# Attention feeding a two-layer feed-forward block on one core: left keys' values in one pass of 64x32 tiles, hand-overs of PSUM banks on SyncE, a new order of the work

## The chip, the core and the metric

The kernel runs on one core of a Trainium2 chip. The metric is the device time of one execution in microseconds (us). Inputs and output lie in HBM. "PE" is TensorE, "DVE" VectorE, "ACT" ScalarE, "POOL" GpSimd and "SP" SyncE; a row with a "q" behind the engine's name belongs to that engine's sequencer, which issues DMAs and semaphore work. PSUM has 8 banks of 128 partitions x 512 float32 values; TensorE writes there.

## The reference

```
# q, k, v: 8 x 12 heads x 448 x 64;  cap = 30
scores = cap * tanh((q @ k^T / sqrt(64)) / cap)
attn   = softmax(scores)                     # over the keys
x      = (attn @ v), heads side by side      # 3584 x 768
out    = max(x @ w1, x @ w2) @ w_out         # w1, w2: 768 x 1024, w_out: 1024 x 768
```

## The kernel before

**The algebra.** max(x w1, x w2) is relu(x (w1 - w2)) + x w2, so that out = relu(x wd) w_out + x wm, with wd = w1 - w2 (`subtract`) and wm = w2 w_out (`premultiply`, from transposed blocks of w2 that `turn_w2` makes). Both are made once, in the first third of the run. |cap x tanh| is at most 30, so exp needs no maximum taken off. Everything that TensorE multiplies is bf16.

**Attention.** The 96 heads are worked in 48 pairs and 24 quads of two pairs (four heads, the token's number t). The 448 keys are three chunks of 128 and 64 left over; all scores are turned round: partitions are keys, the 448 columns are queries.
- `scores` (S, L477): for a pair and a chunk two matmuls of 64x128 tiles, one per head, side by side. `left` (L, L484 to L490): the 64 left keys of all four heads of a quad, four matmuls of 64x64 tiles that run side by side.
- `tanh` (T, L482), `tanh_left` (TL, L494), `ex` (E, L498) and `ex_left` (EL) run on ScalarE: tanh from PSUM, then exp in place.
- `add` (A, L510) and `add_left` (B) on VectorE add the exponentials of the chunks for the sums of softmax, from quad 3 on. `total` (Y, L535) sums over the partitions with a matmul of ones, into a bank of the "mm" set; for quads 0 to 2 it takes the chunks themselves.
- `invert` (Y1, Y2, Y3; L537 to L548): the sums stand 32 times over in partitions; a transpose of 32x32 blocks, a reciprocal of 128 partitions x 14, and a transpose back (L546) give the inverse of every sum in all 32 partitions of its head.
- `values` (V, u = 0 and 1; L552 to L564): 32 of the 64 dims of four heads at a time. L560 takes the three full chunks, twelve 128x32 matmuls of 448 columns, four heads side by side. L564 takes the left keys with 128 rows as well: the left keys of two heads share the partitions, `vl` holds v for one half of the rows and zeros for the other (memsets, L286 and L287), so that the other head's exponentials are multiplied by zero. So it has four 128x32 matmuls for u = 0 and four for u = 1.
- `normalize` (N, L573) on VectorE multiplies by the inverse and writes x, transposed, as chunks `2q + u` of 128 rows.

The scores, the left scores and the values share two slots of PSUM, two banks each, handed out in turn by one pool (`s_psum`, name "s", bufs=2, L249). The quad's values hold one of them until both normalises are done.

**The feed-forward block.** It is cut into groups (`Group`): stage 1 makes one 128-wide slice of relu(x wd) for the 448 tokens of a batch (6 chunks of 128), stage 2 a 128 x 384 piece of the output (14 chunks). Each group has one of four banks ("mm0" to "mm3"; token O opens it) and ends with ev: relu on VectorE (L618), or a copy on VectorE (L651) followed by a store (st, L633). A chunk is done as two matmuls of 64x128 tiles, one for the upper and one for the lower 64 rows. `M x y n` puts n such steps of group x on rows 0 to 63 beside n of group y on rows 64 to 127, so that two groups run side by side. Both halves of a group add to the same bank, one after the other; between them stands a **hand-over** (H, L604 to L607): a no-op on an engine's queue that waits for the last matmul of one half and for which the first matmul of the other half waits. In the program of before the no-ops stand on VectorE.

**Loads and crosses.** k, q, v and the weights are loaded and cast by POOL's queue (lk, lq, lv, lw1, lw2, lwo). `load_wo` (L355 to L360) cuts each half of w_out into WOP pieces; WOP is 1. `x_rows` picks which rows of w1 and w2 make a chunk. For pairs 0 to 9 TensorE transposes q and k (X, Xh); from quad 5 on `cross` (cr, L444) does it with a DMA transpose on SyncE's queue, after q and k of that quad have landed and the scores of the quad two before, which hold the same buffer, are done. SyncE also issues the stores.

**The order.** The kernel schedules by hand (`manual_schedule`): the string ORDER (from L9) lists all steps, the STEPS dict at the end maps tokens to the functions, and each engine gets its instructions in the order in which the string names them. Semaphores between engines are added by the framework. D (`keep_warm`, L436) multiplies constants while nothing else is there.

Of the kernel before, what the change touches and what calls it, by code (L numbers as in the profile page):

```python
# [9 lines left out]
dm; ms0; ld0 k; ld0 q; ms; lk 1 0; id; lwo 0 0; lk 2 0; lq 1 0; lw2 0; cd k; lk 3 0; cd q; lw2 2; D 3 28;  # L10
Xh 0 0 0; Xh 0 1; D 3 8; lq 2 0; lq 3 0; XCh 0 0; XCh 0 1; S 0 0; S 0 1; T 0 0; T 0 1; D 3 8; S 0 2; T 0 2;
lw2 1; E 0 0 3; lwo 1 0; lk 4 0; Xh 1 0 1; D 3 22; Xh 1 1; D 3 14; XC 1; lv 0 0; W 0 2; lv 0 1; L 0; WC 0;
S 1 0; TL 0; lv 0 2; OP 0 0 3; P 0 0 1; W 2 0; T 1 0; lv 0 3; EL 0; S 1 1; lw2 3; WC 2; S 1 2; X 2 1; T 1 1;
X 3 2; XC 2; T 1 2; lv 1 0; W 1 0; XC 3; E 1 0 2; S 2 0; WC 1; S 2 1; P 0 0 7; T 2 0; OP 2 0 1; P 2 0 2;
PC 0 0; P 2 0 3; E 1 2 3; P 2 0 1; S 2 2; P 2 0 2; T 2 1; PC 2 0; T 2 2; lv 1 1; OP 0 1 2; P 0 1 5; lv 1 2;
P 0 1 3; OP 2 1 0; P 2 1 1; lv 1 3; P 2 1 1; PC 0 1; P 2 1 3; lw2 5; L 1; Y 0 3; TL 1; lq 4 0; V 0 0; lw2 4;
Y1 0; E 2 0 3; V 0 1; Y2 0; lq 5 0; Y3 0; S 3 0; lk 5 0; N 0 0; W 3 1; P 2 1 1; N 0 1; lv 2 0; P 2 1 1; T 3 0;
P 2 1 1; OP 1 0 2; P 1 0 1; WC 3; P 1 0 1; lv 2 1; S 3 1; EL 1; P 1 0 1; PC 2 1; lv 2 2; S 3 2; P 1 0 1; T 3 1;
P 1 0 2; lv 2 3; P 1 0 2; OP 1 1 3; P 1 1 1; T 3 2; P 1 1 1; PC 1 0; P 1 1 1; lk 6 0; X 4 1; E 3 0 2; P 1 1 1;
XC 4; P 1 1 4; lk 7 0; S 4 0; PC 1 1; S 4 1; T 4 0; W 4 0; lw1 5; W 5 2; WC 4; E 3 2 3; OP 3 0 1; P 3 0 1;  # L20
lq 6 0; S 4 2; WC 5; X 5 3; T 4 1; lq 7 0; P 3 0 1; XC 5; P 3 0 1; lw1 2; P 3 0 1; T 4 2; P 3 0 2; lw1 0; L 2;
Y 1 0; TL 2; lq 8 0; V 1 0; lq 9 0; Y1 1; E 4 0 3; V 1 1; lw1 3; Y2 1; Y3 1; S 5 0; N 1 0; P 3 0 1; lk 8 0;
P 3 0 1; OP 4 1 2; P 4 1 1; N 1 1; P 4 1 2; T 5 0; P 4 1 1; lw1 1; PC 3 0; X 6 3; EL 2; sub 5 0; lk 9 0; S 5 1;
S 5 2; X 7 0; T 5 1; XC 6; P 4 1 2; T 5 2; XC 7; P 4 1 1; lq 10 0; S 6 0; sub 2 0; P 4 1 1; OP 5 0 1; P 5 0 1;
E 5 0 2; P 5 0 1; S 6 1; P 5 0 2; PC 4 1; P 5 0 1; lw1 4; P 5 0 3; T 6 0; sub 0 1; OP 4 0 3; P 4 0 2; PC 5 0;
P 4 0 3; E 5 2 3; P 4 0 1; S 6 2; P 4 0 2; T 6 1; OP 3 1 0; P 3 1 2; PC 4 0; P 3 1 1; lv 3 0; P 3 1 2; T 6 2;
P 3 1 2; sub 3 0; lv 3 1; L 3; Y 2 2; lv 3 2; TL 3; V 2 0; lv 3 3; Y1 2; E 6 0 3; V 2 1; Y2 2; lk 10 0; Y3 2;
S 7 0; N 2 0; sub 1 1; X 8 1; N 2 1; X 9 3; T 7 0; XC 8; P 3 1 1; EL 3; S 7 1; XC 9; S 7 2; OP 5 1 2; P 5 1 1;
lk 10 1; P 5 1 1; PC 3 1; P 5 1 1; T 7 1; P 5 1 1; A 3 0 1; P 5 1 2; lk 11 0; P 5 1 2; T 7 2; sub 4 0; O 0 1;
M 0 -1 1; lk 11 1; S 8 0; M 0 -1 1; E 7 0 2; M 0 -1 1; S 8 1; PC 5 1; lq 11 0; M 0 -1 3; A 3 0 2; O 1 3;  # L30
M 1 -1 3; lv 4 0; H 0; M 1 0 1; T 8 0; M 1 0 1; A 3 1 1; M 1 0 1; lv 4 1; O 2 0; M 2 0 2; H 1; B 3 0; E 7 2 3;
M 2 0 1; lv 4 2; S 8 2; M 2 1 1; B 3 1; M 2 1 1; T 8 1; M 2 1 1; lv 4 3; O 3 2; M 3 1 1; ev 0; M 3 1 2;
lk 12 0; H 2; T 8 2; A 3 1 2; M 3 2 2; cr 5; M 3 2 1; ev 1; lk 12 1; O 4 1; M 4 2 1; L 4; M 4 2 1; lq 12 0;
TL 4; Y 3 3; V 3 0; Y1 3; E 8 0 3; lk 13 0; V 3 1; Y2 3; Y3 3; lk 13 1; S 9 0; M 4 2 1; N 3 0; M 4 3 1; lv 5 0;
M 4 3 1; N 3 1; M 4 3 1; O 5 3; M 5 3 2; lv 5 1; T 9 0; H 4; M 5 3 1; ev 2; S 9 1; M 5 4 1; lv 5 2; ev 3;
M 5 4 1; EL 4; M 5 4 1; S 9 2; A 4 0 1; lv 5 3; O 6 0; M 6 4 3; T 9 1; H 5; A 4 0 2; M 6 5 1; lq 13 0; M 6 5 2;
ev 4; O 7 2; M 7 5 1; T 9 2; M 7 5 1; S 10 0; lk 14 0; H 6; M 7 5 1; M 7 6 1; E 9 0 2; M 7 6 1; ev 5; S 10 1;
lk 14 1; M 7 6 1; O 8 1; M 8 6 2; H 7; lq 14 0; M 8 6 1; M 8 7 2; ev 6; T 10 0; M 8 7 1; O 9 3; M 9 7 1;
A 4 1 1; M 9 7 1; lk 15 0; M 9 7 1; E 9 2 3; H 8; S 10 2; ev 7; M 9 8 1; lk 15 1; M 9 8 2; B 4 0; M 9 8 1;
T 10 1; M 9 8 1; lq 15 0; cr 6; M 9 8 1; B 4 1; M 9 8 2; T 10 2; M 9 8 2; A 4 1 2; M 9 8 1; O 10 0; M 10 8 3;  # L40
L 5; Y 4 2; TL 5; V 4 0; Y1 4; V 4 1; E 10 0 3; Y2 4; Y3 4; S 11 0; M 10 9 1; lv 6 0; N 4 0; M 10 9 2; M 8 9 1;
N 4 1; M 8 9 1; lv 6 1; M 8 9 2; H 10; M 8 9 1; S 11 1; lv 6 2; T 11 0; A 5 0 1; M 8 9 3; lv 6 3; O 11 2;
M 11 9 1; A 5 0 2; EL 5; M 11 9 1; S 11 2; M 11 9 1; lk 16 0; ev 8; M 11 10 2; T 11 1; M 11 10 1; ev 9;
M 11 10 1; cr 7; M 11 10 1; lk 16 1; M 11 10 2; T 11 2; M 11 10 1; S 12 0; lq 16 0; M 11 10 1; st 0 0;
M 11 10 2; E 11 0 2; O 12 1; M 12 10 1; S 12 1; H 11; M 12 10 1; lk 17 0; M 12 10 1; M 12 11 2; H 10 2;
M 12 11 1; lk 17 1; M 10 11 2; H 12; M 10 11 1; T 12 0; A 5 1 1; M 10 11 2; lq 17 0; M 10 11 2; B 5 0;
M 10 11 1; E 11 2 3; O 13 3; M 13 11 1; S 12 2; M 13 11 1; B 5 1; M 13 11 1; M 13 12 1; T 12 1; M 13 12 1;
ev 10; M 13 12 3; lk 18 0; A 5 1 2; T 12 2; M 13 12 3; ev 11; M 13 12 1; lk 18 1; L 6; Y 5 0; TL 6; V 5 0;
lq 18 0; Y1 5; st 0 1; V 5 1; E 12 0 3; Y2 5; lk 19 0; Y3 5; S 13 0; M 13 12 1; lv 7 0; N 5 0; M 13 12 1;
O 14 2; M 14 12 2; H 13; N 5 1; lv 7 1; M 14 12 1; M 14 13 2; H 12 2; S 13 1; lv 7 2; T 13 0; A 6 0 1;  # L50
M 14 13 1; M 12 13 2; lv 7 3; M 12 13 1; H 14; A 6 0 2; EL 6; M 12 13 1; S 13 2; M 12 13 1; lk 19 1; M 12 13 2;
T 13 1; M 12 13 1; O 15 0; M 15 13 1; cr 8; M 15 13 1; lq 19 0; ev 12; M 15 13 1; M 15 14 1; T 13 2; M 15 14 1;
ev 13; S 14 0; M 15 14 1; O 16 1; M 16 14 1; E 13 0 2; M 16 14 1; H 15; S 14 1; M 16 14 1; st 0 2; M 16 15 2;
ev 14; M 16 15 1; O 17 3; M 17 15 2; H 16; T 14 0; M 17 15 1; A 6 1 1; M 17 16 3; ev 15; O 18 2; M 18 16 1;
E 13 2 3; S 14 2; M 18 16 1; H 17; B 6 0; M 18 16 1; M 18 17 1; T 14 1; M 18 17 1; B 6 1; M 18 17 1; O 19 0;
M 19 17 2; ev 16; T 14 2; M 19 17 1; H 18; ev 17; M 19 18 3; lk 20 0; A 6 1 2; O 20 1; M 20 18 3; lk 20 1; L 7;
ev 18; Y 6 3; TL 7; V 6 0; Y1 6; lq 20 0; V 6 1; E 14 0 3; Y2 6; Y3 6; lk 21 0; S 15 0; M 20 19 1; N 6 0;
lv 8 0; M 20 19 2; N 6 1; O 21 2; M 21 19 2; lv 8 1; M 21 19 1; H 20; S 15 1; T 15 0; ev 19; M 21 20 1; lv 8 2;
M 21 20 2; A 7 0 1; O 22 3; M 22 20 1; lv 8 3; EL 7; M 22 20 1; S 15 2; H 21; A 7 0 2; M 22 20 1; lk 21 1;
M 22 21 2; T 15 1; ev 20; M 22 21 1; O 23 0; M 23 21 1; cr 9; lq 21 0; M 23 21 1; H 22; M 23 21 1; T 15 2;  # L60
M 23 22 1; S 16 0; ev 21; M 23 22 3; E 15 0 2; M 23 22 1; S 16 1; M 23 22 6; O 24 1; M 24 22 1; T 16 0;
M 24 22 1; H 23; A 7 1 1; M 24 22 1; M 24 23 3; H 22 2; E 15 2 3; B 7 0; M 22 23 1; S 16 2; M 22 23 1; H 24;
M 22 23 1; B 7 1; M 22 23 1; T 16 1; M 22 23 3; A 7 1 2; M 22 23 1; lk 22 0; O 25 2; M 25 23 1; T 16 2;
M 25 23 1; ev 22; M 25 23 1; L 8; ev 23; lk 22 1; M 25 24 1; TL 8; Y 7 3; V 7 0; lq 22 0; Y1 7; st 1 3;
E 16 0 3; V 7 1; Y2 7; lk 23 0; Y3 7; S 17 0; M 25 24 1; N 7 0; lv 9 0; M 25 24 3; N 7 1; M 25 24 1; lv 9 1;
M 25 24 2; T 17 0; M 25 24 1; A 8 0 1; S 17 1; lv 9 2; M 25 24 2; O 26 0; M 26 24 1; A 8 0 2; EL 8; M 26 24 1;
lv 9 3; S 17 2; M 26 24 1; H 25; M 26 25 1; lk 23 1; M 26 25 1; T 17 1; H 24 2; M 26 25 1; M 24 25 1; cr 10;
M 24 25 1; H 26; M 24 25 1; lq 23 0; M 24 25 1; T 17 2; M 24 25 1; S 18 0; M 24 25 2; E 17 0 2; M 24 25 1;
S 18 1; O 27 3; M 27 25 1; ev 24; M 27 25 2; M 27 26 2; ev 25; M 27 26 3; T 18 0; M 27 26 1; A 8 1 1;
M 27 26 3; st 1 4; M 27 26 1; B 8 0; E 17 2 3; M 27 26 1; S 18 2; O 28 1; M 28 26 1; H 27; B 8 1; M 28 26 2;  # L70
T 18 1; M 28 27 2; H 26 2; A 8 1 2; M 28 27 1; M 26 27 2; T 18 2; M 26 27 2; lk 24 0; L 9; Y 8 2; TL 9; V 8 0;
# [132 lines left out]
def kernel(  # L204
# [11 lines left out]
    nc = tc.nc  # L216
    f32 = mybir.dt.float32
# [14 lines left out]
    NX = 10  # L232
    KB = 2
    VB = 2
    QB = 2
    NS = 3
    W2T = 4
    WOP = 1
    R7 = S // 64
    OB = 4  # L240
    scale = 1.0 / (D ** 0.5)

    ctx.enter_context(tc.manual_schedule())
    const = ctx.enter_context(tc.tile_pool(name="const", bufs=1))
# [490 lines left out]
```

## Time and profile before

| | before |
|---|---|
| median of 3 runs | 339.29 us (338.48 to 340.11) |
| the profiled execution | 338.55 us |
| its span, first to last instruction | 336.7 us |
| mean granted clock of TensorE | 0.999 |
| TensorE busy | 324.5 us, 96%, 4096 matmuls |
| ScalarE busy | 275.0 us, 82% |
| VectorE busy | 228.6 us, 68% |
| GpSimd busy | 173.5 us, 52% |
| chain that ended last | PE 76%, DMA 10%, DVE 5%, ACT 4% |
| DMA | 45.90 MB, mean 136 GB/s |

The span counts from the first instruction to the last; the execution's time has 1.85 us more around it. Busy time of an engine is the union of its instructions; matmuls that run side by side on different tiles count once there, and in the groups by line each with its own length. In a timeline a row has the start (us from the span's start), the length, the engine, the line, the operation, what it writes and reads, and the number of instructions that it stands for; "[1.54 <-PE s L490]" means that the engine had been idle for 1.54 us until that matmul released it. A group by line has min/median/max ns of one, the time of first and last, and what it waited for.

### The profile page before, as it was taken

The numbers are of one execution on the slowest core, as the hardware profiler recorded it, in microseconds if no ns is written. First come the engines' busy times: TensorE is split into PE (matmuls) and PEld (weight loads), VectorE is DVE, ScalarE is ACT, GpSimd is POOL, SyncE is SP. The second block draws the span as 40 slices with busy tenths as digits, with TensorE's granted clock in tenths as the row PEclk, the third lists the DMA queues.
The fourth block names the chain that finished last, engine by engine and source line by source line (L and its number), as shares of the span: only waits on it lengthen the run. The fifth ranks groups of instructions, "written<-read, shape, count | busy, mean of one in ns | idle before, by whom it ended". The sixth has DMA issues, their size and how long they took to land.

```text
span 336.7 us, 9698 instructions
## 1 busy us (share of the span) xinstructions
PE 324.5 (96%) x4096; PEld 198.0 (59%) x4096; DVE 228.6 (68%) x410; ACT 275.0 (82%) x267; POOL 173.5 (52%) x249
## 2 busy tenths in 40 slices
PE   7799999999999999999999999999999999999994
PEld 6545555555766555656665564557675556559662
DVE  2337779786797659758777768767976678675321
ACT  4879999999989998998899998999899989910000
POOL 6547499967774661792855258398438302000000
PEclk9999999999999999999999999999999999999999
DMA  8999999999999999999999999999999983031033
GB/s 148 204 171 156 256 246 72 151 136 169 159 147 132 140 141 140 182 99 180 187 140 65 133 116 224 132 153 177 144 128 138 182 123 47 2 96 47 2 95 93
DMA packets 136077, 45.90 MB, mean 136 GB/s; under 512 B 116321, under 2 KB 131041, under 8 KB 136033
## 3 DMA queue, kind: packets, MB, share of 16 engines
q0 software_dynamic: 96288, 25.08, 77.7%
q1 hardware_dynamic: 39440, 19.86, 31.1%
q8 instruction: 32, 0.52, 0.7%
q10 hardware_dynamic: 304, 0.33, 0.3%
q14 instruction: 13, 0.10, 0.1%
HBM read 47.45 MB, written 11.01 MB: 174 GB/s over the span
## 4 chain that ended last, share of the span: by engine, by line
PE 76%; DMA 10%; DVE 5%; ACT 4%; issue 2%; POOL 0%; SPq 0%; POOLq 0%; DVEq 0%; ACTq 0%
PE mm L597 49%; PE s L477 8%; PE s L560 6%; DMA wo_sb<-in_moe_w_out_dram 5%; PE mm L402 4%; DMA qkT<-kqs 4%; ACT e L498 3%; PE s L490 2%; PE s L564 2%; PE mm L535 1%; PE mm L592 1%; DMA out_dram<-osb 1%; ACT e L482 1%; PE mm L429 1%; DVE osb L651 1%
## 5 line engine op out<-in xcount | busy, mean ns | idle before, releaser
L482 ACT ACTIVATE e<-s 128x896 bf16<-128x896 f32 x144 | 127.5, 930 | 1.9 <-PE s L477 1.9
L498 ACT ACTIVATE e<-e 128x2688 bf16<-128x2688 bf16 (+2 forms) x72 | 122.9, 1708 | 0.0
L597 PE MATMUL mm<-wo_sb,gT 64*128 64x384 bf16 x864 | 116.2, 323 | 0.0
L597 PE MATMUL mm<-wm_sb,xT 64*128 64x384 bf16 x648 | 102.1, 323 | 0.0
L597 PE MATMUL mm<-xT,wd_sb 64*128 64x448 bf16 x768 | 98.9, 349 | 1.0 <-DVE gT L618 0.8
L328 POOL DMA_DIRECT2D kqs<-in_k_dram x76 | 55.8, 737 | 71.3 <-DMA qkT<-kqs 68.7
L597 PEld LDWEIGHTS <-gT 64*128 64x128 bf16 x864 | 60.4, 94 | 24.0 <-issue 0.4
L597 PEld LDWEIGHTS <-wd_sb 64*128 64x128 bf16 x768 | 55.4, 94 | 20.8 <-issue 2.4
L597 PEld LDWEIGHTS <-xT 64*128 64x128 bf16 x648 | 51.0, 94 | 18.4 <-issue 1.0
L477 PE MATMUL s<-qkT 64*128 64x448 bf16 x288 | 55.4, 354 | 2.2 <-ACT e L482 1.8
L618 DVE TENSOR_SCALAR gT<-mm 128x448 bf16<-128x448 f32 x64 | 39.5, 622 | 13.6 <-PE mm L597 13.1
L651 DVE COPY osb<-mm 128x384 f32<-128x384 f32 x54 | 29.7, 555 | 24.3 <-PE mm L597 23.2
L510 DVE TENSOR_TENSOR esum<-e 128x896 bf16<-128x896 bf16 x42 | 26.1, 621 | 23.9 <-ACT e L498 18.3
L346 POOL DMA_DIRECT2D vp<-in_v_dram x48 | 30.4, 638 | 22.0 <-PE s L564 15.9
L328 POOL DMA_DIRECT2D kqs<-in_q_dram x38 | 36.9, 972 | 4.3 <-PE mm L402 3.1
L560 PE MATMUL s<-e,vp 128*32 128x448 bf16 x576 | 35.7, 352 | 0.0
L494 ACT ACTIVATE el<-s 128x896 bf16<-128x896 f32 x24 | 22.0, 917 | 16.4 <-PE s L490 15.9
L477 PEld LDWEIGHTS <-qkT 64*128 64x128 bf16 x288 | 17.2, 94 | 26.7 <-issue 13.8
L661 ACT COPY osb<-mm 128x192 f32<-128x192 f32 x1 | 0.3, 319 | 36.5 <-DMA out_dram<-osb 36.5
L346 POOL DMA_DIRECT2D vl<-in_v_dram x48 | 29.4, 620 | 0.6 <-PE s L477 0.5
L573 DVE TENSOR_TENSOR xT<-s,inv 128x448 bf16<-128x448 f32 x48 | 27.8, 620 | 2.6
L510 DVE TENSOR_TENSOR esum<-esum,e 128x896 bf16<-128x896 bf16 x42 | 26.2, 624 | 1.8
(56 smaller groups left out, 265.8 us busy)
## 6 DMA issues: line engine op xcount, KB each, us to landing
out_dram<-osb SPq DMA_DIRECT2D x54, 192.0 KB, 4.2
vp<-in_v_dram POOLq DMA_DIRECT2D x38, 160.0 KB, 5.3
kqs<-in_q_dram POOLq DMA_DIRECT2D x47, 112.0 KB, 5.7
kqs<-in_k_dram POOLq DMA_DIRECT2D x76, 56.0 KB, 4.0
osb<-in_moe_w_dram POOLq DMA_DIRECT2D x4, 512.0 KB, 9.1
wo_sb<-in_moe_w_out_dram POOLq DMA_DIRECT2D x2, 768.0 KB, 9.2
gT<-in_moe_w_dram POOLq DMA_DIRECT2D x6, 256.0 KB, 7.4
xT<-in_moe_w_dram POOLq DMA_DIRECT2D x2, 512.0 KB, 6.2
```

The source lines that it names most:

```text
L328: nc.gpsimd.dma_start(out=to, in_=x)
L346: nc.gpsimd.dma_start(out=to, in_=x)
L477: nc.tensor.matmul(s[:, h, :S], k_of(t, o, h, j), q_of(t, o, h))
L482: nc.scalar.activation(expo[i][:, 2 * j : 2 * j + 2, :], slots[i, j][:, :, :S], AF.Tanh, scale=scale / cap)
L494: nc.scalar.activation(left_e[t], slots[t][:, :, :S], AF.Tanh, scale=scale / cap)
L498: nc.scalar.activation(e, e, AF.Exp, scale=float(cap))
L510: nc.vector.tensor_add(d, e[:, 0:2, :] if j == 1 else d, e[:, 2 * j : 2 * j + 2, :])
L560: nc.tensor.matmul(ps[r, u, :S], vp[t % VB][:, m, j if turned_by_pe(t) else 2 * j, u::2], expo[2 * t + o][:, 2 * j + h, :], start=(j == 0) ...
L573: nc.vector.tensor_mul(x, vals[t][:, u, :S], sums[t, 3])
L597: ins = nc.tensor.matmul(self.ps, w[r], x[r], start=first, stop=self.at == [self.n, self.n]).ins
L618: nc.vector.tensor_relu(gT[b // 2][:, f, cs], ps)
L651: nc.vector.tensor_copy(o[:, hs], ps)
```

## The change

- **Left values.** `values_left` (VL) does the left keys of a quad for both u in one go: eight matmuls of 64x32 tiles, four heads times two halves of the dims, each with the 64 rows of its own head, into eight different places of 64 rows x 32 columns of the array. It comes ahead of the full chunks and starts the sums (start=True); `values` only adds (start=False) and takes chunks j0 to j1. So `vl` needs no zeros, and its memsets go.
- **Places.** For that to fit, u = 1 has its heads' results in other partitions: `place(m, u)` is R32[m ^ 2u], lower and upper 64 partitions exchanged. Odd chunks of x therefore have their halves exchanged, and so must the rows of w1 and w2: `load_rows` loads the odd chunks in two DMAs of 64 rows. The inverses are needed in both arrangements: Y2b copies the reciprocals with the halves exchanged (two copies of 64 partitions x 14 on VectorE), Y3b is a second transpose of 32x32 blocks.
- **Left scores** are eight 64x32 tiles as well, instead of four 64x64.
- **Slots.** The two PSUM slots of scores and values have names, and which step takes which is written down (TURN), not handed out in turn.
- **Hand-overs** are no-ops on SyncE, not on VectorE.
- **w_out** comes in four DMAs (WOP = 2), not two.
- **keep_warm** keeps a bank that nobody else took (`idle`).
- **ORDER** is new throughout: another front (the first 20 us), other places for the groups' steps, hand-overs and crosses, VL and the split values in the quads, and 134 hand-overs instead of 131. A quad of both orders (quad 6's cross; quad 4's values):

```
before:  M 9 8 1; T 10 1; M 9 8 1; lq 15 0; cr 6; M 9 8 1; B 4 1; M 9 8 2; T 10 2; M 9 8 2; A 4 1 2; M 9 8 1;
         O 10 0; M 10 8 3; L 5; Y 4 2; TL 5; V 4 0; Y1 4; V 4 1; E 10 0 3; Y2 4; Y3 4; S 11 0; M 10 9 1; lv 6 0;
         N 4 0; M 10 9 2; M 8 9 1; N 4 1;
after:   M 8 6 1; H 7; cr 6; lk 15 1; S 10 2; B 4 0; M 8 6 1; M 8 7 1; E 9 2 3; M 8 7 1; B 4 1; lq 15 0; M 8 7 1;
         O 9 1; M 9 7 2; H 8; ev 6; M 9 7 1; T 10 2; M 9 8 2; A 4 1 2; M 9 8 2; L 5; ev 7; VL 4; TL 5; Y 4 3;
         V 4 0 0 2; Y1 4; V 4 1 0 2; E 10 0 3; V 4 0 2 3; Y2 4; V 4 1 2 3; Y3 4; S 11 0; M 9 8 1; lv 6 0; M 9 8 1;
         Y2b 4; M 9 8 1; N 4 0; M 9 8 2; lv 6 1; M 9 8 2; Y3b 4;
```

The diff, without the order's text:

```diff
-    WOP = 1
+    WOP = 2
...
-    s_psum = ctx.enter_context(tc.tile_pool(name="s_psum", bufs=2, space=PSUM))
+    s_psum = ctx.enter_context(tc.tile_pool(name="s_psum", bufs=1, space=PSUM))
...
     def fill_const(eng, i):
-        eng.memset(vl[i][64:, 0::3, :], 0.0)
-        eng.memset(vl[i][:64, 1:3, :], 0.0)
...
+    def load_rows(eng, to, w, c):
+        x = w.rearrange("(q p u) n -> q u p n", p=P, u=2)[c // 2, c % 2]
+        if c % 2 == 0:
+            eng.dma_start(out=to, in_=x)
+            return
+        for r in (0, 64):
+            eng.dma_start(out=to[r : r + 64], in_=x[64 - r : 128 - r])
...
     def keep_warm(bank, n):
-        ps = mm_tile(bank)
+        if bank not in idle:
+            idle[bank] = mm_tile(bank)
         for _ in range(n):
-            nc.tensor.matmul(ps[:, :P], warm, warm, start=True, stop=True)
+            nc.tensor.matmul(idle[bank][:, :P], warm, warm, start=True, stop=True)
...
+    TURN = (0, 1, 0, 1, 1, 0)
+
+    def s_tile(turn, t):
+        return s_psum.tile([P, 2, 512], f32, name=f"s{turn ^ (t % 2)}")
...
-        s = slots[i, j] = s_psum.tile([P, 2, 512], f32, name="s")
+        s = slots[i, j] = s_tile(TURN[o * NJ + j], t)
...
     def left(t):
-        s = slots[t] = s_psum.tile([P, 2, 512], f32, name="s")
+        s = slots[t] = s_tile(1, t)
         for o in range(2):
             for h in range(2):
-                r = slice(64 * (h ^ o), 64 * (h ^ o) + 64)
-                nc.tensor.matmul(s[r, o, :S], k_of(t, o, h, NJ), q_of(t, o, h))
+                for p in range(2):
+                    r = slice(64 * (h ^ o) + 32 * p, 64 * (h ^ o) + 32 * p + 32)
+                    nc.tensor.matmul(s[r, o, :S], k_of(t, o, h, NJ)[:, 32 * p : 32 * p + 32], q_of(t, o, h))
...
-            rs = sums[t, 2] = att.tile([P, NB, 1], f32, name="rs", bufs=2)
-            nc.vector.reciprocal(rs, sums[t, 1][:, :, 0:1])
+            rs = sums[t, 2, u] = att.tile([P, NB, 1], f32, name=f"rs{u}", bufs=2)
+            st = sums[t, 1][:, :, 0:1]
+            if u == 0:
+                nc.vector.reciprocal(rs, st)
+            else:
+                nc.vector.tensor_copy(rs[64:], sums[t, 2, 0][:64])
+                nc.vector.tensor_copy(rs[:64], sums[t, 2, 0][64:])
         else:
-            inv = sums[t, 3] = att.tile([P, S], f32, name="inv", bufs=2)
+            inv = sums[t, 3, u] = att.tile([P, S], f32, name=f"inv{u}", bufs=2)
...
+    def place(m, u):
+        return R32[m ^ (2 * u)]
+
+    def values_left(t):
+        ps = vals[t] = s_tile(0, t + 1)
+        for m, (o, h) in enumerate(heads(t)):
+            r = slice(64 * (h ^ o), 64 * (h ^ o) + 64)
+            for u in range(2):
                 nc.tensor.matmul(
-                    ps[r, u, :S], vp[t % VB][:, m, j if turned_by_pe(t) else 2 * j, u::2], expo[2 * t + o][:, 2 * j + h, :], start=(j == 0), stop=False
+                    ps[place(m, u), u, :S], vl[t % VB][r, m, u::2], left_e[t][r, o, :], start=True, stop=False
                 )
-        for m, ((o, h), r) in H:
-            nc.tensor.matmul(ps[r, u, :S], vl[t % VB][:, m, u::2], left_e[t][:, o, :], start=False, stop=True)
+
+    def values(t, u, j0, j1):
+        for j in range(j0, j1):
+            w = vp[t % VB][:, :, j if turned_by_pe(t) else 2 * j, u::2]
+            for m, (o, h) in enumerate(heads(t)):
+                nc.tensor.matmul(
+                    vals[t][place(m, u), u, :S], w[:, m, :], expo[2 * t + o][:, 2 * j + h, :], start=False, stop=(j == NJ - 1)
+                )
...
-        nc.vector.tensor_mul(x, vals[t][:, u, :S], sums[t, 3])
+        nc.vector.tensor_mul(x, vals[t][:, u, :S], sums[t, 3, u])
...
         def hand_over(self):
-            self.turn = nc.vector.nop().ins
+            self.turn = nc.sync.nop().ins
             tc.add_manual_dep(self.turn, self.last[1].name, BANK, reason="bank")
```

## The prediction

> **What bounds the kernel now.** I read the profile's first part, then busy time by stretch, then the chain, then rows for the tiles the change touches.
>
> ```profile
> PE 324.5 (96%) x4096; PEld 198.0 (59%) x4096; DVE 228.6 (68%) x410; ACT 275.0 (82%) x267; POOL 173.5 (52%) x249
> ```
>
> TensorE is busy 96% of the span of 336.7 us; ScalarE follows. By stretch (columns: length, then busy us of PE, PEld, DVE, ACT, POOL):
>
> ```profile
> 25.00:59.00 34.00, 33.98 (x480) 18.45 (x470) 27.29 (x45) 33.48 (x34) 26.90 (x40) 1.00 1.06 181
> 59.00:299.00 240.00, 237.44 (x2978) 143.18 (x2976) 180.02 (x321) 224.58 (x217) 132.03 (x182) 1.00 1.23 137
> ```
>
> From 25 to 59 us ScalarE has no slack: the first values matmuls of quads 0 to 3 stand at 24.83, 36.35, 47.82 and 59.34, 11.5 us apart. From 59 to 299 a quad takes 12.0 us, of which ScalarE fills 11.2: here TensorE sets the pace, and a wait of TensorE is paid in full, because after 299 it alone works until 332. The clock granted is 1.00 throughout.
>
> **Part 1, the pass saved.** TensorE's timeline at quad 0:
>
> ```profile
> 24.83 0.74 PE L560 MATMUL s<-e,vp 128*32 128x448 bf16 x12
> 25.40 0.36 PE L564 MATMUL s<-el,vl 128*32 128x448 bf16 x4
> 25.59 0.74 PE L560 MATMUL s<-e,vp 128*32 128x448 bf16 x12
> ```
>
> Four 128x32 tiles side by side make a pass: three passes from 24.83 to 25.40, one from 25.40 to 25.59, 0.19 us each. The left keys have two passes a quad; in the change eight 64x32 tiles make one. 24 x 0.19 = **-4.5 us**. The left scores become eight tiles too, still one pass. The number of changes of tile shape per quad stays three, so I cost that at nothing.
>
> The Trainium skill (PSUM — Partial Sum Buffer, PSUM bank collisions raise a hardware error) says that different row tiles can't write the same PSUM bank at the same time; the eight tiles do that, in disjoint partitions. By it the two row halves would take turns, two passes, and this part would bring 0 instead of -4.5. The trace speaks against a price of that kind: L490 already does this with four 64x64 tiles, starts at 12.76, and the next pass starts at 13.07: 0.31, of which about 0.12 is the change of shape (the same gap stands between L564's last pass and the scores, 26.16 to 26.45). One pass, then.
>
> **Part 2, the front.** ScalarE's timeline:
>
> ```profile
> 9.21 2.44 ACT L498 ACTIVATE e<-e 128x2688 bf16<-128x2688 bf16 x1
> 13.19 0.92 ACT L494 ACTIVATE el<-s 128x896 bf16<-128x896 f32 x1 [1.54 <-PE s L490]
> 24.19 0.92 ACT L494 ACTIVATE el<-s 128x896 bf16<-128x896 f32 x1 [1.97 <-PE s L490]
> 25.00 2.44 ACT L498 ACTIVATE e<-e 128x2688 bf16<-128x2688 bf16 x1
> ```
>
> The second gap exists because TensorE, ahead of L 1, waits for the second half of w_out (landed 21.49). The new order puts ahead of L 1 only premultiplies that need the first quarter, so 1.97 goes. The first gap: k of pair 1 now lands behind a quarter of w_out. The first half took 5.2 us beyond the landing before it, a quarter 2.6, so k 1 lands near 7.7 us and the first exp starts 0.5 later, but L 0 is then ready and tanh of the left keys starts near 12.1 instead of 13.19; the next scores wait for its slot, 0.5. In sum exp of pair 2 starts near 22.4 instead of 25.0, -2.6. But by quad 3 the new order has done 1.9 us less of work that must be done at some time (17 fewer premultiply matmuls of 0.17 before quad 0, one w2 transpose of 0.5 more, the rest made up partly by quad 3). Net **-0.6**; bounds +1.9 (ScalarE no earlier) and -1.5 (also the slot wait gone and another 0.4). Cutting the odd rows of w1 and w2 in two adds DMA issues of 0.57 on POOL, which is idle half the time and waits for landings; no bytes are added: 0.
>
> **Part 3, the hand-overs.** In one PSUM bank the lower and the upper row half of a group take turns; a no-op between them waits for the last matmul of one half, and the first of the other waits for the no-op. 131 of them stand on VectorE, 134 would stand on SyncE, in program order between crosses (DMA transposes) and stores. Rows of the operations by line (min/median/max ns):
>
> ```profile
> L606 DVEq EVENT_SEMAPHORE  x131: 21/21/21, 54.8 to 325.1; - x131
> L444 SPq DMA_TRANSPOSE qkT<-kqs x19: 1472/1982/3723, 59.1 to 268.6; - x19
> L633 SPq DMA_DIRECT2D out_dram<-osb x46: 466/588/1462, 77.7 to 328.4; - x46
> ```
>
> The no-op itself is nothing. But a cross keeps SyncE 1.5 to 3.7 us, and what follows starts only then:
>
> ```profile
> 75.45 2.18 SPq L444 DMA_TRANSPOSE qkT<-kqs  x1
> 77.68 0.60 SPq L633 DMA_DIRECT2D out_dram<-osb  x1
> ```
>
> 75.45 + 2.18 = 77.63, and the store starts at 77.68. It isn't a wait counted as issue: the last scores matmul that this cross waits for ended at 75.42.
>
> So I walked the changed SyncE order: for each of the 19 crosses, the passes from the matmul that releases it to the first matmul that needs the next hand-over. In seven there is room (19 to 26 passes). In twelve there are few: quad 6: 10 passes; quads 9, 15, 21: 8; 10, 16, 22: 7; 11, 17, 23: 11; 12, 18: 9. At 0.19 for 448 columns (above) and 0.167 for 384 (the chain's last piece, 28 matmuls in 4.67) that is 1.9, 1.5, 1.2, 1.9 and 1.7 us, together 19.1. Needed each time: the issue, mean 2.16 (the 19 add up to 41.0), and about 0.3 for a matmul's tail (0.36 long in a pass of 0.19) and three hops of 0.03 to 0.05. 12 x 2.46 - 19.1 = 10.4. After crosses 11, 17 and 23 two stores (0.5 and 0.6) stand between two hand-overs that are three passes apart: 3 x 0.6 = 1.8. In sum **+12.2**. Behind the stalled matmul is TensorE's whole queue, and ScalarE waits for scores in it. Bounds: all issues at their shortest, +2; all at their longest, +31; if the no-op alone counts, at best -0.8, what TensorE waits for relu results on VectorE today. I take the mean of 19 issues, because the new ones start at the same place, behind the last scores of a quad.
>
> The Trainium skill (DMA: Bandwidth & Descriptors, Issuing engines are not separate DMA queues) says that starting a DMA costs the sequencer a time usually small against the transfer. At a price like a plain store's 0.5 the twelve gaps would suffice, and this part would be 0. The trace has 1.98 of issue against 7.2 to landing.
>
> **Part 4, VectorE.** Per quad one more 32x32-block transpose (L546: 0.65) and two copies of 64x14. No row shows these; nearest are a memset of 64 rows, 0.11, and the reciprocal of 128x14, 0.24; I take 0.11, since no division is in it. 24 x 0.87 = 21 more, 131 x 0.021 = 3 fewer: 229 to 247 us, still under TensorE. It counts where the scores wait for a slot: from the sums' last pass to the second normalise 0.2 + 0.65 + 0.24 + 0.65 + 0.22 + 0.62 + 0.65 + 0.6 (a relu between) + 0.62 = 4.45, against 4.2 to 4.3 us of passes ahead of the scores that need the slot. About 0.2 x 20 = **+4**; bounds 0 and +9 (copies at 0.24). The present order has waits as well: its quads from 59 to 299 stand 5.7 us behind their passes at the best quad's rate (0.5 of lost starts each). I let 4 of these go with the old order: **-4**, bounds 0 and -5.7.
>
> **Sum.** -4.5 - 0.6 + 12.2 + 4 - 4 = +7.1. The profiled execution took 338.55 (span 336.7 and 1.85 around it): 345.7. It lies 0.74 under the median of 339.29, so 346.4; I say **346**, about 2% slower.
>
> **Rivals.**
> - SyncE goes on while a cross's descriptors are made, or the issue shrinks to a store's 0.5, and the kernel does what it says; it decides at an issue of about 1.3 us. Parts 3 and 4 fall to 0: 338.55 - 5.1 = 333.4, so 334.2. For: TensorE's pace is real and the pass goes. Against: the two rows at 75.45 and 77.68, and a shortest issue of 1.47. Chance 0.22, one in seven of it within 0.5%.
> - The eight tiles take two passes (the change's gain does not come): forecast + 4.5 = 350.5. Against: L490. Chance 0.08.
> - VectorE takes the bound: copies at 0.24 put 0.45 instead of 0.2 into each quad, and its later evictions hold the four PSUM banks of the groups: +5 to +8, so 351 to 354. For: 86% busy from 80 to 100 us. Against: 75% over 59 to 299. Chance 0.12.
> - The forecast: 0.58, with its own range 341.5 to 350, an eighth of it within 0.5%.
>
> **Range and chances.** Without the first rival over 2 in 10 are left out, so the range reaches to it: 334 to 353. 0.5%, about what a measurement here can tell from no change, is 1.7 us. Faster 0.19; same 0.03 + 0.07 = 0.10; slower 0.71.
>
> **What would show it.** SyncE: hand-overs of about 0.02 us starting right behind a cross, and TensorE idle before matmuls of the groups with SyncE as releaser, some 0.5 to 1.5 us at quads 9 to 12, 15 to 18, 21 to 23, none at 7, 8, 13, 14. Passes: left values and left scores 0.19 each. Front: exp of pair 2 near 22.4. Wrong if the cross's rows stay at 1.5 to 3.7 and no TensorE gap follows them, or if gaps stand before scores with VectorE's normalise as releaser.

## The result and the profile after

The changed kernel takes 358.98 us (median of 4) beside 339.7 for the one before on the same chip: ratio 1.055, 95% interval 1.050 to 1.061. It is slower, as forecast, but by 19 us where the forecast had 7. The first profile of it is of a disturbed execution, so the lines below are from a second one of the same kernel (span 357.6 us; the run again, below), and where this document gives a ratio it is of undisturbed executions alone, while a median is of all.

Its first part, engines' busy time and share of the span:

```profile
PE 330.5 (92%) x4202; PEld 195.3 (55%) x4202; DVE 249.3 (70%) x478; ACT 277.0 (77%) x267; POOL 174.8 (49%) x257
```

TensorE falls from 96% to 92%. To see where, take the stretch from the first values matmul of quad 4 to that of quad 23. It holds 19 quads, and neither the front nor the tail. Before, then after (columns: length, then busy us of PE, PEld, DVE, ACT, POOL):

```profile
70.90:299.31 228.41, 225.90 (x2839) 136.74 (x2834) 170.62 (x303) 213.29 (x206) 121.58 (x168) 1.00 1.22 137
```

```profile
76.29:319.18 242.89, 229.10 (x2918) 132.19 (x2914) 187.07 (x360) 214.77 (x206) 118.98 (x168) 1.00 1.15 128
```

The stretch is 14.5 us longer, although it holds fewer passes: counted from the program, 2.9 us less of TensorE's time. TensorE's idle time rises from 2.5 to 13.8 us. The rest is in its busy time (225.9 to 229.1): a pass starts 0.17 to 0.2 us after the one before, but a matmul lasts 0.33 to 0.39 (rows below), so a start that is a little late leaves no idle time. What ends the idle time stands in TensorE's list of waits (total us, times, longest):

```profile
PE mm L639 <- SPq L648: 10.5, 13, 1.9
PE s L506 <- DVE xT L615: 2.0, 7, 0.4
```

L648 is the hand-over's no-op, L615 the normalise. Such a wait from close by, SyncE's timeline and TensorE's, at the cross of quad 16:

```profile
197.00 2.69 SPq L468 DMA_TRANSPOSE qkT<-kqs  x1
```

```profile
199.80 0.33 PE L639 MATMUL mm<-wo_sb,gT 64*128 64x384 bf16 x1 [1.91 <-SPq L648]
```

197.00 + 2.69 = 199.69: the hand-over comes when the cross has been issued, and TensorE starts 0.11 later, having idled 1.91. The rows of both by line (min/median/max ns) show that the no-op itself takes 17 ns, and that the crosses are about what they were:

```profile
L648 SPq EVENT_SEMAPHORE  x134: 17/17/17, 61.2 to 345.9; - x134
```

```profile
L468 SPq DMA_TRANSPOSE qkT<-kqs x19: 1481/2157/2691, 61.8 to 287.8; - x19
```

The pass itself is there. TensorE at quad 14:

```profile
204.67 0.39 PE L520 MATMUL s<-qkT 64*32 64x448 bf16 x8
204.87 0.37 PE L596 MATMUL s<-el,vl 64*32 64x448 bf16 x8
205.37 1.31 PE L604 MATMUL s<-e,vp 128*32 128x448 bf16 x24
```

Eight left scores from 204.67 to 204.87, so one pass of 0.20 us. Eight left values and the four matmuls of the sums fill the 0.50 to 205.37: two passes and one change of shape.

### The profile page after: what moved, and what is told of

Same layout as the page of the kernel before. It is cut to its first block, busy times and chain, and to the rows that moved or that the text cites. A ratio compares the mean times of both kernels' runs of the same rounds, so it can differ in the third digit from the quotient of the medians.

```text
span 360.7 us, 9976 instructions
## 1 busy us (share of the span) xinstructions
PE 329.5 (91%) x4202; PEld 193.9 (54%) x4202; DVE 249.8 (69%) x478; ACT 277.4 (77%) x267; POOL 174.7 (48%) x257
## 4 chain that ended last, share of the span: by engine, by line
PE 58%; DVE 24%; DMA 6%; SPq 5%; issue 4%; POOL 2%; ACT 0%; POOLq 0%; DVEq 0%
PE mm L639 43%; DVE inv L581 6%; PE s L506 6%; DVE xT L615 5%; DVE st L570 3%; SPq L468 3%; DMA gT<-in_moe_w_dram 2%; DMA wo_sb<-in_moe_w_out_dram 2%; PE mm L425 2%; PE mm L565 2%; PE s L520 2%; DVE esum L540 2%; SPq L675 2%; DMA vp<-in_v_dram 1%; DVE rs L575 1%
## 5 line engine op out<-in xcount | busy, mean ns | idle before, releaser
L639 PE MATMUL mm<-wo_sb,gT 64*128 64x384 bf16 x864 | 118.3, 325 | 6.5 <-SPq L648 6.5
L639 PE MATMUL mm<-wm_sb,xT 64*128 64x384 bf16 x648 | 105.4, 323 | 2.4 <-SPq L648 2.1
L639 PE MATMUL mm<-xT,wd_sb 64*128 64x448 bf16 x768 | 101.1, 352 | 6.4 <-SPq L648 4.4
L343 POOL DMA_DIRECT2D kqs<-in_k_dram x76 | 54.6, 720 | 87.4 <-DMA qkT<-kqs 85.9
L343 POOL DMA_DIRECT2D kqs<-in_q_dram x38 | 35.2, 926 | 0.4 <-issue 0.4
L506 PEld LDWEIGHTS <-qkT 64*128 64x128 bf16 x288 | 18.1, 94 | 27.0 <-issue 20.8
L604 PE MATMUL s<-e,vp 128*32 128x448 bf16 x576 | 31.6, 352 | 0.0
L581 DVE STREAM_TRANSPOSE inv<-rs 128x448 f32<-128x448 f32 x48 | 30.7, 640 | 0.8
L615 DVE TENSOR_TENSOR xT<-s,inv 128x448 bf16<-128x448 f32 x48 | 29.6, 617 | 0.8
```

Source lines behind the costliest of these rows:

```text
L343: nc.gpsimd.dma_start(out=to, in_=x)
L506: nc.tensor.matmul(s[:, h, :S], k_of(t, o, h, j), q_of(t, o, h))
L581: nc.vector.transpose(inv.rearrange("p (b c) -> p b c", c=32), sums[t, 2, u].to_broadcast([P, NB, 32]))
L604: nc.tensor.matmul(vals[t][place(m, u), u, :S], w[:, m, :], expo[2 * t + o][:, 2 * j + h, :], start=False, stop=(j == NJ - 1))
L615: nc.vector.tensor_mul(x, vals[t][:, u, :S], sums[t, 3, u])
L639: ins = nc.tensor.matmul(self.ps, w[r], x[r], start=first, stop=self.at == [self.n, self.n]).ins
```

## The experiments

In each, only what the diff shows is changed. "L520" and the like are lines of the changed kernel.

**again**: the changed kernel unchanged.

> The changed kernel once more, for a profile beside the others. All theories: 357 to 360 us. In its profile the matmuls that need a hand-over behind a cross should again stand late, 15 us in sum over the 19 crosses as in the first profile of it, and the scores 7 us later in sum than before.

Measured 359.6. For each hand-over in its trace I took the time that TensorE lost just before the first matmul that needs it: 12.8 us behind the 19 crosses, 4.0 behind stores, 4.0 over the other 91, which is 0.04 each. Cross by cross, the lost time in the main follows the room: 2.1 at quad 16 and 1.5 at quad 22 (7 passes of room), 0.1 at quads 8, 14 and 20 (19 passes and more).

**hand_dve**

```
-            self.turn = nc.sync.nop().ins
+            self.turn = nc.vector.nop().ins
```

> The changed kernel with the hand-overs back on VectorE, nothing else. Theory Q (the crosses and stores on SyncE's queue hold the hand-overs): its profile put 15.2 us before matmuls whose hand-over stands behind a cross and 3.5 behind two stores, so 359 - 18.7 + 1 = 341 to 343 us. Rival V (VectorE's added work and the new order are the main price, and a stall that goes at a hand-over comes back as a wait of the scores for the normalise): 350 us or more.

Measured 347.1 (ratio to before 1.021, 1.014 to 1.027), its six runs between 343.6 and 349.7. The queue is worth 12.6 us by the medians and 13.4 by the ratios (1.060 against 1.021), but it is not all: 7 to 8 us stay, so both theories hold a part. Its stretch from quad 4 to 23:

```profile
74.46:303.80 229.34, 225.93 (x2919) 137.40 (x2914) 185.28 (x361) 213.79 (x206) 119.02 (x168) 1.00 1.19 135
```

**before_sync**: the kernel before with `nc.sync.nop()`.

> The kernel before with the hand-overs on SyncE, nothing else. Theory Q: in this order 8 crosses leave only 6 to 10 passes (11.0 us in all) before a matmul that needs the next hand-over; the profile of the changed kernel shows that 2.75 us are needed each time, so 22 - 11 = 11, and four more crosses with 2.0 to 2.6 us of room give about 2: 339.5 + 13 = 352 us (349 to 355). Rival V: the queue alone costs little, 340 to 344 us.

Measured 358.1 (ratio 1.055). Theory Q holds, but its price was set too low, 13 us where 18.8 came: in the trace 19.9 us are lost behind crosses. Part of that is one cross that took long, and all of it was paid (SyncE's timeline, then TensorE's):

```profile
127.52 4.01 SPq L444 DMA_TRANSPOSE qkT<-kqs  x1
```

```profile
131.64 0.50 PE L597 MATMUL mm<-wo_sb,gT 64*128 64x384 bf16 x1 [3.92 <-SPq L606]
```

**no_second_inverse** (the exchange of the inverses is left out):

```
-        nc.vector.tensor_mul(x, vals[t][:, u, :S], sums[t, 3, u])
+        nc.vector.tensor_mul(x, vals[t][:, u, :S], sums[t, 3, 0])
...                                    # Y2b and Y3b do nothing
```

> The changed kernel without Y2b and Y3b (the two copies and the second transpose, 21 us of VectorE): both normalises of a quad use the first inverse, so the odd chunks get the inverses of the wrong heads. Hand-overs stay on SyncE. Theory V: the 7 us more that the scores wait go, 352 +- 2 us. Theory Q: the hand-overs hold as before, and what VectorE gains is lost at the next one: 357 to 359 us.

Measured 353.7: 6.0 us less than again, as theory V said. The lost time behind crosses was still 13.2 us, so what the queue costs does not come from the second inverse.

**cross_later**: 12 crosses moved like this one, one to three hand-overs on.

```
-cr 15; O 52 2; ... H 51; ... H 52;
+O 52 2; ... H 51; ... H 52; cr 15;
...
```

> The changed kernel, hand-overs still on SyncE, but each of the 12 crosses that stood right ahead of a pressing hand-over (quads 6, 9 to 12, 15 to 18, 21 to 23) is put one to three hand-overs later in the order, where 18 to 27 passes of TensorE lie ahead of the next one. Theory Q (it is the cross's issue in SyncE's queue): of the 12.8 us before matmuls behind crosses about 11 go, 359.6 - 11 = 349 us (347 to 351). Rival (the hand-overs are late on SyncE anyway, or the crosses then land late and the scores of their quad wait): 356 us or more, with waits of the scores for a DMA.

Measured 352.2 (ratio 1.030, 1.022 to 1.038), its four runs between 347.9 and 354.8. By the medians 7.4 us of the expected 11 came, by the ratios (1.060 against 1.030) 10, with hand-overs still on SyncE. That the issue of the cross ahead of the hand-over is the cause is confirmed.

**dve_no_second_inverse**: both edits, hand_dve and no_second_inverse.

> Hand-overs on VectorE, without Y2b and Y3b: both normalises use the first inverse, so odd chunks get the inverses of the wrong heads. Theory V: the same 6 us as with the hand-overs on SyncE (359.6 to 353.7), so 341 us (340 to 343). Rival (the 6 us were there because late hand-overs and late normalises delay each other): 344 to 347 us.

Measured 338.6, ratio to before 0.996 (0.992 to 0.999). VectorE's added work is worth 8.5 us here, more than the 6.0 with the hand-overs on SyncE; the expectation had 6 again. In the same way the queue is worth 15.1 us without the second inverse (353.7 - 338.6), and 12.6 with it. So neither price can be given without saying what else is in the kernel. Without the queue and without the second inverse the change is level with before, not 4.5 us faster:

```profile
73.90:299.00 225.10, 223.19 (x2919) 133.36 (x2914) 169.66 (x304) 213.17 (x206) 118.97 (x168) 1.00 1.23 138
```

225.10 against 228.41 before: here the stretch gains 3.3 us, of which the passes are 2.9. The front gives it back (below).

**dve_split_normalise** (hand_dve, and):

```
+        for r in (0, 64):              # u == 1, in place of Y2b and Y3b
+            nc.vector.tensor_mul(x[r : r + 64], vals[t][r : r + 64, u, :S], sums[t, 3, 0][64 - r : 128 - r])
```

> Hand-overs on VectorE, and no second inverse: the second normalise is cut in two of 64 partitions, each of which reads the first inverse from the other half. VectorE per quad: two copies (0.34) and a transpose (0.64) go, one more normalise (0.62) comes. Theory V (the added work ahead of the second normalise costs, also without the queue): 347.1 - 2 = 345 us (343.5 to 346). Rival (with the hand-overs off SyncE VectorE has room again): 347 us.

Measured 347.7, no gain. VectorE's timeline at quad 14 tells why:

```profile
199.21 0.62 DVE L616 TENSOR_TENSOR xT<-s,inv 128x448 bf16<-128x448 f32 x1 [0.16 <-DVE inv L581]
200.26 0.63 DVE L540 TENSOR_TENSOR esum<-e 128x896 bf16<-128x896 bf16 x1 [0.42 <-ACT e L528]
200.92 1.26 DVE L619 TENSOR_TENSOR xT<-s,inv 64x448 bf16<-64x448 f32 x2
```

In the order an add of exponentials stands between the two normalises. VectorE reaches it early, waits 0.42 for ScalarE, adds, and only then normalises. What was saved ahead of the add went into this wait, and the second normalise behind it takes 1.26 instead of 0.61.

**split_normalise_first** and **dve_normalise_first**: the second normalise goes ahead of that add, in the kernel with halves, and in the one with two inverses.

```
-N 14 0; ... A 15 0 1; ... N 14 1;
+N 14 0; N 14 1; ... A 15 0 1;         # with two inverses: Y3b 14; N 14 1;
```

> Hand-overs on VectorE, no second inverse, the second normalise in two halves as in the run before, but right behind the first normalise, ahead of the adds, which there held VectorE by 0.42 of idling and 0.66 at quad 14. Theory V2: second normalise 1.1 us earlier than in that run and 0.9 earlier than with two inverses, so nearly the time without a second inverse: 347.7 - 7 = 341 us (339.5 to 343). Rival: 346 to 348 us.

> Hand-overs on VectorE, both inverses kept, and in the order the second normalise of each quad stands right behind the second transpose, ahead of the add of exponentials that stood between them (0.5 to 0.6 us a quad). Theory V2 (what counts is when the second normalise ends, since the scores wait for its slot): the 6 us of waits ahead of scores behind the values fall by about 3, 347 - 3 = 344 us (342 to 345.5). Rival (VectorE's total work counts, the order of it does not): 346.5 to 348 us.

With halves 343.6: 4.1 us less, the fastest version that keeps the exchange, and still 1.4% over before (1.012 to 1.017). With two inverses 350.8, 3.7 us more than hand_dve, a miss. There the waits of the scores for the normalise are gone from TensorE's list (0.7 us in hand_dve's), but this stands in it, where hand_dve's has no wait for a hand-over and 0.3 us for a relu:

```profile
PEld L643 <- DVEq L652: 7.7, 14, 1.1
PE mm L643 <- DVE gT L664: 2.3, 6, 0.4
```

L652 is the hand-over, now on VectorE, and L664 the relu at a group's end. The moved normalise stands right behind its transpose, and the no-ops and relus behind both in VectorE's queue come later: the price of SyncE's crosses again, on another queue. That this is the whole of the 3.7 us is argued from the list, not shown by a run.

**split_first_k1_first**: `lk 1 0` ahead of `lwo 0 0`.

> The run before, with the load of k of pair 1 put ahead of the first quarter of w_out. The third scores of pair 0 waited for that k (1.1 to 1.9 us of idle TensorE at 8 to 9 us in all profiles of the new front). If that wait is part of the front's price: 1 to 1.5 us less than the run before. Rival (ScalarE or the w_out quarter, which then lands later, takes it over): within 0.7 us of it.

Measured 343.6, the same: the rival.

**dve_subtract_on_vector**: `sub 0 1; sub 1 1` become `sub 0 0; sub 1 0`.

> Hand-overs on VectorE, and the two subtracts of w1 - w2 that GpSimd did are done by VectorE as well. In the profile with hand-overs on VectorE a copy of 64x14 took 1.48 us at 50.09 instead of 0.17, and ended when GpSimd's subtract (49.38 to 51.53) did; TensorE then idled 1.59. If GpSimd's subtract holds up VectorE: the copy is at 0.17, VectorE has 2.4 us more to do, and the time is 1 us less, 346 us. If the copy was late for another reason, it stays long, and the time is 347 to 349 us.

Measured 347.7 against 347.1: no gain. The copy is short again (longest 0.55), but VectorE now has 2.4 us of subtracts to do as well. The last section returns to the copy.

**Old order.** Four kernels have the order, front and `WOP = 1` of before, hand-overs on VectorE, and the new left scores and left values with what these need (places, rows of w1 and w2). Their edit in the order:

```
-L 11; ... Y 10 0; TL 11; V 10 0; Y1 10; ... V 10 1;
+L 11; ... VL 10; Y 10 0; TL 11; V 10 0 0 3; Y1 10; ... V 10 1 0 3;
```

> The order and front of before, w_out in two pieces, hand-overs on VectorE, but left scores and left values as in the change (eight 64x32 tiles, one pass), and no second inverse, so odd chunks get the inverses of the wrong heads. The pass by itself: 339.3 - 24 x 0.19 = 335 us (334 to 336). Rival (the new order and front, not VectorE, are what hides the pass, or the eight tiles cost as much as two passes): for the first, this run is 3.5 us under the new order without a second inverse (338.6); for the second, it is 339 or more.

> The run before with the second inverse in the order right behind the first: all of the change but its order, its front, its slots and the hand-overs. Theory V (two copies and a transpose cost what lies ahead of the second normalise, whatever the order): 335 + 8.5 = 343.5 us (341 to 347). Rival (8.5 us was a matter of the new order): 335 to 338 us.

> Old order, one pass, and instead of a second inverse the second normalise in two halves of 64 partitions (0.62 more a quad, directly ahead of the scores that wait for its slot). Theory V: 0.62 x 20 is paid in part, as with the new order (343.6 against 338.6, 5 us): 340 us (338 to 342). Rival (the old order has room): 335 to 337 us, the best kernel.

> The run before with the changed kernel's fixed PSUM slots, in which the second scores of the odd pair take the slot of the first ones instead of that of the values, so that only the third wait for the second normalise. If what costs is the wait for the values' slot, it is 2 to 4 us under the run before; if the scores then wait for tanh instead, the same or more.

Measured 345.0, 359.7, 355.8 and 356.7 against 339.6 before: the first three missed, on the slow side, and the fourth is the second case of its expectation. The pass alone, with one inverse for both, is 5.4 us *slower* than before; a second inverse adds 14.7 to that, the halves 10.8. The waits of the first, and those of before:

```profile
PEld L496 <- DVE xT L605: 11.7, 18, 0.9
PE s L496 <- DVE xT L605: 5.2, 19, 0.6
```

```profile
PEld L477 <- DVE xT L573: 6.1, 20, 0.5
```

The waiting matmuls are the second scores of an odd pair, which need the slot that the normalise before frees. In the old order the left values stood between the sums and these scores. Now they stand ahead of the sums, so two passes of cover (0.38) are gone behind the sums while VectorE's chain is as long as ever. Over 24 quads that is 9.1 us, an estimate; 345.0 lies 9.9 above 339.6 - 4.5. Fixed slots change nothing, 356.7 and 355.8, but they were no test of this wait: at quad 14 of that trace the tanh that the second scores then wait for ends at 205.58 + 0.91 = 206.49, and the second normalise at 205.26 + 1.26 = 206.52.

**Later scores.** The last three move `S 2t+1 1` back in the old order, behind 3 passes of the groups, up to 5, and 6 to 8:

```
-N 10 1; ... H 40; S 23 1; T 23 0; A 11 0 1; M 38 39 1; lv 12 2; M 38 39 3;
+N 10 1; ... H 40; T 23 0; A 11 0 1; M 38 39 1; lv 12 2; M 38 39 2; S 23 1; M 38 39 1;
```

> The run old_order_one_pass (old order and front, one pass, no second inverse, so wrong inverses for odd chunks), with the second scores of every odd pair three passes of the groups later from quad 4 on. Theory C (the saved pass stood between the sums and the scores that wait for the normalise, so that the wait grew by what was saved): the wait falls back to that of before, and the pass shows: 345 - 6 = 339, or 336 if the first quads keep up too (335 to 340). Rival (the loss has nothing to do with these scores): 344 to 346 us.

> old_order_split (355.8) with the second scores of odd pairs up to 5 passes later. Theory C: the second normalise ends 0.62 later than with one inverse for both, 5 passes are 0.85 us, so about the time of old_order_one_pass or less: 340 to 346 us. Rival: 354 to 357 us.

> The same with the second scores 6 to 8 passes later and the third ones 3. Theory C: the wait for the second normalise is covered, 337 to 341 us, unless ScalarE, which then gets these scores later, falls behind: then waits of tanh for scores, and 342 to 348 us.

Measured 339.5 (ratio 1.004, 1.001 to 1.007), 345.6 and 346.6. Theory C holds for the first two: three passes of cover bring 5.5 us back, five bring 10 to the kernel with halves. In the first one's list TensorE's wait is nearly gone (0.6, where the weight loads of before have 6.1):

```profile
PEld L498 <- DVE xT L607: 0.6, 2, 0.3
```

The third brings no more, in the way that the expectation allowed: its list has 7.2 us of tanh waiting for scores, where before has 1.9 and the second one 5.1.

No version that keeps the exchange of the halves beats the kernel before.

## Why the prediction was right and wrong

The direction was right, and the rival with the largest chance (SyncE not blocking) is refuted. The size was not: 6.7 us forecast, 19.3 measured. Nearly all that is missing lies in two terms that I had put near nothing, VectorE (0 in sum) and the front (-0.6). By the steps:

- **Part 3, hand-overs: right.** Forecast +12.2, measured 12.6 (again against hand_dve; 13.4 by the ratios). The places are the forecast ones: quad 8, which had room, lost 0.1, quads 16 and 22, which had least, 2.1 and 1.5. In the trace of again the terms are 11.8 at the twelve pressed crosses, where I had 10.4, and 3.0 at the stores behind crosses 11, 17 and 23 (hand-overs 32, 66 and 100: 1.3, 0.9 and 0.7), where I had 1.8. So these terms lose 14.8 in the trace where 12.6 is paid; where the rest is hidden is not settled. That the sum came so near is in part luck: the same kind of working gave 13 us for before_sync, where 18.8 came.
- **Part 4, VectorE: the step that failed.** I set +4 for the longer chain and let -4 of old waits go with the old order, so nothing in sum. The old waits did not go: with hand-overs and second inverse out of the way the stretch from quad 4 to 23 gained 3.3 us, 2.9 of them passes, so 0.4 and not 4. And the chain is worth 8.5 us, not 4 (hand_dve against dve_no_second_inverse, medians; their profiles differ by 5.6). For a quad I had counted it well. Here is quad 14 of hand_dve, the first values, the second normalise and the third scores of the pair, which need its slot:

```profile
195.03 1.31 PE L604 MATMUL s<-e,vp 128*32 128x448 bf16 x24
```

```profile
198.88 0.61 DVE L615 TENSOR_TENSOR xT<-s,inv 128x448 bf16<-128x448 f32 x1
```

```profile
199.54 0.37 PE L506 MATMUL s<-qkT 64*128 64x448 bf16 x2
```

  The values start at 195.03, when the sums' pass is over, and the normalise ends at 199.49: 4.46, where I had 4.45. Over the stretch the two kernels differ by 229.34 - 225.10 = 4.2, which is the forecast 4. What I left out lies outside it: in these profiles quads 0 to 3 take 1.5 us more with the second inverse (50.9 against 49.4), 1.3 of it in quad 2, where one copy took 1.48 instead of 0.17 (last section), and what comes behind quad 23 takes 0.8 more (38.4 against 37.6). Why the medians differ by more than the profiles is not settled. The copies took 0.17, where I had taken 0.11 and that rival 0.24; its +5 to +8 for VectorE was the better size. The sign of being wrong that I had named came too: TensorE's list in again has 2.0 us of scores waiting for the normalise.
- **Part 2, the front: wrong, -0.6 forecast, about +3.7 measured**, which is what lies between 339.35 - 4.5 and dve_no_second_inverse's 338.6. The first half came only in part (and its -2.6 and +1.9 add up to -0.7). Exp of pair 2, which I had near 22.4, starts at 23.04 in hand_dve, 23.98 in dve_no_second_inverse, 26.15 in again and 26.56 in cross_later, against 25.00 before: in some runs of the new front earlier, in others later. And I took ScalarE's 11.5 us a quad as given for quads 0 to 3. In dve_no_second_inverse they take 49.4 us instead of 46.1, with about as much for TensorE to do (17 premultiply matmuls more; ten steps of groups, four passes of values and one w2 transpose fewer). Here is the third of them, from the values of quad 2 to those of quad 3, and in it one row each of VectorE, GpSimd and TensorE:

```profile
49.24:62.12 12.88, 11.32 (x156) 5.57 (x152) 12.35 (x18) 11.01 (x12) 11.72 (x15) 1.00 1.11 111
```

```profile
52.78 3.05 DVE L540 TENSOR_TENSOR esum<-e 128x896 bf16<-128x896 bf16 x1
```

```profile
53.19 2.14 POOL L396 TENSOR_TENSOR wd_sb<-osb,gT 128x1024 bf16<-128x1024 f32 x1
```

```profile
55.39 0.36 PE L639 MATMUL mm<-xT,wd_sb 64*128 64x448 bf16 x1 [1.02 <-POOL wd_sb L396]
```

  VectorE is busy 12.35 of 12.88 us, and TensorE, with 1.56 us idle, no longer keeps ScalarE fed. But VectorE's load is not what ended that idle time: 1.02 of the 1.56 end with GpSimd's subtract (53.19 + 2.14 = 55.33), for which the first matmul of a group waits. And 2.4 of VectorE's 12.35 us belong to one add that took 3.05 instead of 0.61 beside the same subtract. In quad 0, which is 1.0 us longer than before, VectorE is busy only 6.55 of 12.53 us. So in quad 2 the wait for the subtract is the larger part of what this profile shows, and for the other quads the cause stays open. No run moved the subtract within the order; giving both to VectorE, and loading k of pair 1 earlier, brought nothing.
- **Part 1, the pass: right as a count, and it says less than it seems.** 24 passes are gone, the eight tiles run as one. In the stretch of dve_no_second_inverse they are gained, but no run is faster than before by more than 0.4%: the pass in the old order has 345.0, and 339.5 with three passes of groups put in front of the scores, level with before. (There quads 4 to 23 take 227.1 us instead of 228.4, but they begin 2.6 us later.) I read the Trainium skill (PSUM — Partial Sum Buffer, PSUM bank collisions raise a hardware error) as if two row halves that write one bank would take turns. It quotes that different row tiles are not able to access the same PSUM bank at the same time, but the case that it has measured is one bank and the same 32 partitions. Here the tiles write disjoint partitions, and the 0.20 us of the eight left scores above leave no room for turns.
- **Sum of the measured terms:** passes -4.5, front +3.7, hand-overs +12.6, VectorE +8.5 = 20.3, the distance of again from before. The front's term is the rest of this sum; that there is such a loss shows in the 3.4 us by which quads 0 to 3 are longer.

## What to carry to other kernels

A no-op that hands over between two engines costs what stands ahead of it in its queue: ask for the longest instruction there, its room in passes, and everything behind the waiting one. Taking a pass away gains only if it did not cover a chain of another engine that is as long as before; if it did, move other work into its place. When a chain grows, follow it through the real queue, with each instruction in it that waits for a third engine, and into the stages ahead of and behind the steady one. And do not book old waits as a gain unless you can name the step of the new order that takes them away: here 0.4 of 4 us went.

## What the runs showed of the hardware

A small copy on VectorE waited for GpSimd. In the profile of hand_dve (GpSimd's row, then VectorE's), the copy of 64x14 has 1.48 us instead of 0.17:

```profile
49.38 2.15 POOL L396 TENSOR_TENSOR wd_sb<-osb,gT 128x1024 bf16<-128x1024 f32 x1
```

```profile
50.09 1.48 DVE L577 COPY rs<-rs 64x14 f32<-64x14 f32 x1
```

50.09 + 1.48 = 51.57, GpSimd's subtract ends at 51.53. In the kernel before, two normalises ran beside GpSimd's subtract in 1.16 us, as always. They read one operand from PSUM. The Trainium skill (SBUF — State Buffer, Who interferes with whom) says that a copy can enter a mode in which it needs the ports that VectorE shares with GpSimd, and that an instruction with at most one SBUF input does not contend outside such modes. These rows agree with it. The add of two SBUF operands shown for the front was held in the same way: it ended at 55.83, 0.50 behind the subtract.

A normalise of 64 partitions takes about 0.62 us, as one of 128 does (1.26 for two halves above), so cutting it in halves doubles its price. And the issue of a cross has a wide spread, 1.47 us (the shortest of before) to 4.01 (in before_sync), and what stands behind it in the queue waits that long.
